# A convolution branch rewritten: Toeplitz images of all lags, or a chunked scan of states

## The chip, the cores and the metric

The kernel runs on one core of one Trainium2 chip. A core has a matrix engine (PE, with its weight loads PEld shown apart), a vector engine (DVE), a scalar engine (ACT), a general engine (POOL) and a queue engine that issues transfers (SP). 16 DMA engines move data between HBM and the on-chip memory SBUF; PE writes its results to the small memory PSUM. The metric is the time of one execution on the device in microseconds (us), here a median of three runs. The profile is taken of one execution by the hardware's own profiler.

## The reference

A forward pass and its gradients, of two branches that read the same x and are mixed by a gate. Branch a is attention with 32 heads of 18; branch b is a convolution over the 2048 tokens, channel by channel, whose kernel K is a sum of 128 complex exponentials:

```python
def _B_ref(u, A_re, A_im, B_re, B_im, C_re, C_im, log_dt, Dskip):
    dt = jnp.exp(log_dt)[:, None]
    logdA = dt * A                       # A = A_re + 1j * A_im, 576 channels x 128
    dB = dt * Bc
    P = jnp.exp(logdA[:, :, None] * l[None, None, :])      # l = 0 .. 2047
    K = jnp.einsum("dn,dnl,dn->dl", Cc, P, dB).real
    ...                                  # y = causal convolution of K and u, by FFT
    y = (lambda x, *d: x.transpose(*d))(y, 0, 2, 1) + u * Dskip[None, None, :]
    return y

x = A_x
g = _sigmoid((x * gate_w).sum(-1, keepdims=True))
a = _A_ref(x, A_wqkv, A_wo)
b = _B_ref(x, B_A_re, ...)
return g * a + (1 - g) * b
```

What is returned is this output and the gradient for each of the twelve inputs other than B_u. For branch b, with gy = (1 - g) * grad_out, that means: y from K and x; dx, the same convolution run backwards over gy; dK, the correlation of gy with x at each lag; and from dK the gradients of A, B, C and log_dt, which need two sums for each of 576 x 128 states: of dK times the exponential (S0) and of dK times lag times the exponential (S1).

## The kernel before, in words

The program is written with a framework that allocates tiles from pools, adds the semaphores, and orders each engine's instructions by its own planning; only attention has its order written out by hand. Each pool is closed before the next stage's is opened, so that stages take the same SBUF one after the other. All transfers are issued from SP's queue, in order. `mm` (line 30) is the helper behind nearly all matmuls, so they all have line 30.

The stages, by their pools:

- s1 and attention (lines 93 to 491), projections and their gradients (lines 496 to 632). The weight wo is loaded once, in s1, and kept.
- Parameters (lines 681 to 752): dt, A, B and C are transposed so that a state index lies on each partition and a channel in each column; W = C * B * dt and G, the 128th power of the state's factor, are computed; A * dt, once in its own units and once in turns, goes to a DRAM table `ath_d`.
- HX (lines 754 to 818), the gradient of the lags. gy is reversed within each 128 tokens into `GYREVp`, x is reversed and stored to `xpR_d`. For each of the 576 channels `HX`, a 128 x 2048 Toeplitz image of x, is read back from DRAM with overlapping rows (512 KB), and 16 matmuls with 128 x 128 weights and 16 columns accumulate dK for all 2048 lags.
- E (lines 820 to 941), in 36 groups of 16 channels. `abuf` and `thb` (1 MB each) bring A * dt to all partitions; ACT and DVE make the real and imaginary part of the exponential for 128 lags, `E1e` (partition = lag, 16 x 128 columns for each part). PE transposes it (line 889), ACT copies the result out (line 890). Kernel values at lag l + 128 * k are made by two matmuls a channel against a table of W times G to the power k (`Rre`, `Rni`), are transposed and stored to `Kpad_d`. `Vps` multiplies E1e with dK; a 16-step scan in G (lines 926 to 936) makes S0 and S1.
- HK (lines 943 to 994), the outputs. For each channel `HK`, a 128 x 2048 Toeplitz image of K, is read from DRAM (512 KB); each of its 16 blocks serves two matmuls of 16 columns, one for y, one for dx.
- Final (lines 996 to 1104): gradients of the parameters, then two loops over the 16 token tiles for the output and for dx.

The tiles abuf, thb, mag, uk, frac and frac2 of stage E come from a pool with one buffer each; E1e and E1n have two.

Of the kernel before, what the change touches and what calls it, by code (L numbers as in the profile page):

```python
# [17 lines left out]
P = 128  # L18


def build(tc, aps, dbg_aps=None, stages=("s1", "attn", "post", "s4", "final")):
# [39 lines left out]
    with ExitStack() as gctx:  # L61
# [14 lines left out]
        wo_sb = const.tile([P, DC, D], BF, name="wo_sb")  # L76
# [16 lines left out]
        with ExitStack() as ctx:  # L93
# [395 lines left out]
        if "post" in stages:  # L489
# [6 lines left out]
            with ExitStack() as ctx:  # L496
# [3 lines left out]
                OT = pa.tile([P, DC, S], BF, name="OT")  # L500
                cnt = 0
# [132 lines left out]
        if "s4" in stages:  # L634
# [3 lines left out]
            L = S  # L638
            NB = L // P
            LP = L + 2 * P  # L640
            NL1 = L // P
            GS = 16
            NGS = D // GS
            CG = 32
            NCG = D // CG
            HG = 128
            GPB = HG // GS
            INV2PI = float(1.0 / (2.0 * np.pi))
            Kpad_d = dram.tile([D, LP], BF, name="Kpad_d")
            xpR_d = dram.tile([D, LP], BF, name="xpR_d")  # L650
            ath_d = dram.tile([2, D, N], F32, name="ath_d")
            dkk_d = dram.tile([P, D * 2 * NL1], BF, name="dkk_d")
            dkk_v = dkk_d.rearrange("p (d a b) -> p d a b", d=D, a=2)
# [4 lines left out]
            Dskip_b = s4c.tile([P, D], F32, name="Dskip_b")  # L658
            gate_b = s4c.tile([P, D], F32, name="gate_b")
# [3 lines left out]
            Wr_n = s4c.tile([P, D], F32, name="Wr_n"); Wi_n = s4c.tile([P, D], F32, name="Wi_n")  # L663
            Gr_n = s4c.tile([P, D], F32, name="Gr_n"); Gi_n = s4c.tile([P, D], F32, name="Gi_n")
            S0r = s4c.tile([P, D], F32, name="S0r"); S0i = s4c.tile([P, D], F32, name="S0i")
            S1r = s4c.tile([P, D], F32, name="S1r"); S1i = s4c.tile([P, D], F32, name="S1i")
            dDs_row = s4c.tile([1, D], F32, name="dDs_row")
            zero_bf = s4c.tile([P, P], BF, name="zero_bf")
            nc.vector.memset(zero_bf, 0.0)
# [6 lines left out]
            lidx_i = s4c.tile([P, NL1], mybir.dt.int32, name="lidx_i")  # L676
            nc.gpsimd.iota(lidx_i, pattern=[[P, NL1]], base=0, channel_multiplier=1)
            lval = s4c.tile([P, NL1], F32, name="lval")
            nc.vector.tensor_copy(lval, lidx_i)

            with ExitStack() as ctx:
                pp = ctx.enter_context(tc.tile_pool(name="s4pp", bufs=2))
                pps = ctx.enter_context(tc.tile_pool(name="s4pps", bufs=2, space=bass.MemoryType.PSUM))
                for src_ap, dst, fn in ((log_dt, dt_b, "exp"), (Dskip, Dskip_b, None), (gate_w, gate_b, None)):
                    tmpb = pp.tile([P, D], BF, tag="rowb", name="rowb")
                    row = src_ap.rearrange("(o d) -> o d", o=1)
                    nc.sync.dma_start(tmpb, row.to_broadcast([P, D]))
                    if fn == "exp":
                        nc.scalar.activation(dst, tmpb, ACT.Exp)
                    else:  # L690
                        nc.vector.tensor_copy(dst, tmpb)
# [27 lines left out]
                t1 = pp.tile([P, D], F32, tag="t1", name="t1")  # L719
                nc.vector.tensor_tensor(Wr_n, Cr_n, Br_n, op=A.mult)  # L720
                nc.vector.tensor_tensor(t1, Ci_n, Bi_n, op=A.mult)
                nc.vector.tensor_tensor(Wr_n, Wr_n, t1, op=A.subtract)
                nc.vector.tensor_tensor(Wr_n, Wr_n, dt_b, op=A.mult)
# [96 lines left out]
            with ExitStack() as ctx:  # L820
# [8 lines left out]
                for gi in range(NGS):  # L829
# [53 lines left out]
                    if gi == 0:  # L883
                        dbg("E1e0", E1e)
# [267 lines left out]
```

## Time and profile before

| | |
|---|---|
| three timed runs, median | 6802.83 us (6802.13 to 6807.21) |
| the profiled execution, its own time | 6800.58 us |
| its span, first to last instruction | 6798.7 us |
| PE busy | 4762.3 us (70%) |
| DVE busy | 4011.0 us (59%) |
| ACT busy | 3479.8 us (51%) |
| POOL busy | 101.5 us (1%) |
| moved by DMA | 827.93 MB, mean 122 GB/s |

The page's second part cuts the span into 40 equal slices of 170 us and gives a digit for each engine: its busy share in tenths. A group line reads: line, engine, operation, output<-inputs, shape, count | busy time, mean ns of one | idle time of the engine before it, and what ended it. The view of windows gives each engine's busy time in stretches of the span. A timeline line gives the start, the length, and the instruction. A row of transfers gives the size of one in KB and the median time from issue to landing.

### The profile page before, as it was taken

The page shows a single profiled execution, that of the slowest core. Times are in us where ns is not written, and L with a number is a line of the kernel's source. Part 1 is how long each engine was busy: PE and PEld are TensorE (multiplying, and loading weights), DVE is VectorE, ACT ScalarE, POOL GpSimd, SP SyncE. Part 2 cuts the span into 40 slices and gives each one's busy share as a digit, 9 for nine tenths or more (in the row PEclk, how much of TensorE's full clock was granted, in tenths as well). Part 3 has the DMA queues.
Part 4 walks back from the last instruction along what each step waited for, and adds up shares of the span by engine and source line. Part 5 has one row for each costly group of instructions (what it writes and reads, how often), then busy time and mean ns, then how long its engine had stood idle before and what let it go on. Part 6 is the DMA issues. An engine that isn't in the chain of part 4 may idle for free. (4 is left out here: it accounts for less than half of the span.)

```text
span 6798.7 us, 147781 instructions
## 1 busy us (share of the span) xinstructions
PE 4762.3 (70%) x62071; PEld 2257.4 (33%) x62071; DVE 4011.0 (59%) x7837; ACT 3479.8 (51%) x6912; POOL 101.5 (1%) x133
## 2 busy tenths in 40 slices
PE   6779999999999999999979544443322232577672
PEld 4541212121212121222167433332322231466661
DVE  4328999989898989899943500002678767200005
ACT  3347878878787878786833300001866685300001
POOL 1000000000000000000000000000000000000000
PEclk6555555555555555555578655555555555555555
DMA  2130000000001010000030399997322232599996
GB/s 82 63 105 6 6 16 12 6 22 6 22 1 27 1 26 1 17 3 4 3 121 30 95 383 380 379 381 283 115 74 73 70 109 67 210 378 377 374 371 173
DMA packets 370257, 827.93 MB, mean 122 GB/s; under 512 B 163506, under 2 KB 193332, under 8 KB 359732
## 3 DMA queue, kind: packets, MB, share of 16 engines
q1 hardware_dynamic: 369588, 818.48, 33.7%
q8 instruction: 485, 7.95, 0.5%
q14 instruction: 184, 1.51, 0.1%
HBM read 755.45 MB, written 62.92 MB: 120 GB/s over the span
## 5 line engine op out<-in xcount | busy, mean ns | idle before, releaser
L398 DVE TENSOR_TENSOR ds<-ps_P3D,eb 128x512 bf16<-128x512 f32 x2048 | 1293.3, 686 | 128.3 <-PE ps_P3D L30 83.7
L398 DVE TENSOR_TENSOR ds<-ps_P,PT 128x512 bf16<-128x512 f32 x2048 | 1288.3, 686 | 101.5 <-PE ps_P L30 97.0
L394 ACT ACTIVATE eb<-ps_P3S 128x512 bf16<-128x512 f32 x2048 | 1109.2, 596 | 259.8 <-PE ps_P3D L30 179.1
L390 ACT ACTIVATE PT<-ps_P 128x512 bf16<-128x512 f32 x2048 | 1107.8, 596 | 211.9 <-PE ps_P L30 113.4
L30 PE MATMUL ps_P3D<-VaT_g,dOaT_g 19*128 19x512 bf16 x2048 | 790.8, 593 | 16.4 <-DVE ds L398 15.8
L30 PE MATMUL ps_P<-dOaT_g,VaT_g 19*128 19x512 bf16 x2048 | 757.9, 592 | 0.0
L30 PE MATMUL ps_P<-QaT_g,KaT_g 19*128 19x512 bf16 x2048 | 676.0, 597 | 72.1 <-DMA KaT_g<-KaT_d 37.7
L30 PE MATMUL ps_P3S<-KaT_g,QaT_g 19*128 19x512 bf16 x2048 | 671.0, 597 | 31.0 <-ACT eb L394 28.5
L889 PE MATMUL pt_e<-ident_bf,E1e 128*128 128x128 bf16 x1152 | 186.5, 281 | 690.1 <-ACT E1n L890 348.8
L30 PE MATMUL dkps<-GYREVp,HX 128*128 128x16 bf16 x9216 | 343.2, 175 | 456.4 <-DMA HX<-xpR_d 456.4
L30 PE MATMUL dxps<-CXG,HK 128*128 128x16 bf16 x9216 | 545.4, 174 | 145.7 <-issue 143.3
L30 PE MATMUL accA<-PT,Vtok_g 128*32 128x512 bf16 x2048 | 625.0, 608 | 6.0 <-DMA Vtok_g<-Vtok_d 5.8
L30 PE MATMUL accB<-ds,Qtok_g 128*32 128x512 bf16 x2048 | 626.7, 608 | 0.0
L30 PE MATMUL accA<-eb,dOa 128*32 128x512 bf16 x2048 | 626.7, 608 | 0.0
L30 PE MATMUL accB<-ds,Ktok_g 128*32 128x512 bf16 x2048 | 625.2, 608 | 0.0
L30 PEld LDWEIGHTS <-HK 128*128 128x128 bf16 x18432 | 528.3, 104 | 264.8 <-DMA HK<-Kpad_d 144.2
L30 PE MATMUL yps<-CXG,HK 128*128 128x16 bf16 x9216 | 549.9, 175 | 79.5 <-DMA HK<-Kpad_d 77.5
L984 DVE CAST y_tok<-yps 128x512 bf16<-128x512 f32 x18 | 44.0, 2443 | 746.6 <-PE dxps L30 663.8
L816 DVE TENSOR_TENSOR dkk_st<-dkps,lval 128x512 bf16<-128x512 f32 x18 | 12.4, 692 | 784.8 <-DMA HX<-xpR_d 618.5
L30 PEld LDWEIGHTS <-HX 128*128 128x128 bf16 x9216 | 290.7, 105 | 509.5 <-DMA HX<-xpR_d 508.5
L986 ACT CAST dxr<-dxps 128x512 bf16<-128x512 f32 x18 | 10.5, 585 | 795.4 <-PE dxps L30 795.4
L815 ACT CAST dkk_st<-dkps 128x512 bf16<-128x512 f32 x18 | 10.5, 585 | 786.7 <-PE dkps L30 741.9
(306 smaller groups left out, 6195.1 us busy)
## 6 DMA issues: line engine op xcount, KB each, us to landing
HX<-xpR_d SPq DMA_DIRECT2D x576, 512.0 KB, 9.6
HK<-Kpad_d SPq DMA_DIRECT2D x576, 512.0 KB, 6.7
abuf<-ath_d SPq DMA_DIRECT2D x36, 1024.0 KB, 4.7
thb<-ath_d SPq DMA_DIRECT2D x36, 1024.0 KB, 4.9
x_tok<-in_A_x_dram SPq DMA_DIRECT2D x3, 2304.0 KB, 9.5
go_t<-in_grad_out_dram SPq DMA_DIRECT2D x48, 144.0 KB, 2.2
dqkv_d<-dtk SPq DMA_DIRECT2D x48, 144.0 KB, 3.6
dqkv_tok<-dqkv_d SPq DMA_DIRECT2D x1, 6912.0 KB
```

What stands on the lines that cost most here:

```text
L30: return nc.tensor.matmul(out, lhsT=lhsT, rhs=rhs, start=start, stop=stop, **kw)
L390: nc.scalar.activation(out, ps, ACT.Exp)
L394: nc.scalar.activation(out, ps, ACT.Exp)
L398: nc.vector.tensor_tensor(out, ps, e, op=A.mult)
L815: nc.scalar.copy(dkk_st[:, :, 0, :], dkps)
L816: nc.vector.tensor_tensor(dkk_st[:, :, 1, :], dkps, lval.unsqueeze(1).to_broadcast([P, CG, NB]), op=A.mult)
L889: nc.tensor.transpose(pt[:, ri, :], E1e[:, ch, ri, :], ident_bf)
L984: nc.vector.tensor_copy(y_tok[:, :, d0:d0 + CG].transpose([0, 2, 1]), yps)
L986: nc.scalar.copy(dxr, dxps)
```

## The change

The tokens are cut into 16 chunks of 128. Within a chunk, and from each chunk to the next through the 128 complex states, the convolution is computed exactly; only the first 128 lags are needed as a kernel. The convolution part is replaced whole. In order:

- Parameters. x is reversed within each chunk (a matmul with the exchange matrix J for each half of 576 columns) and stored to `xr_d`. `zpow` makes the factor z and its 128th power Z; 14 tables go to `par_d`.
- M, the first 128 lags of dK. Tokens are regrouped as 128 runs of 16. In three batches of 192 channels, `xs` gets eight copies of x, the copy dl shifted by dl partitions (eight loads, of 128 - dl partitions); masks clear what crossed a chunk's start. For each channel one matmul of 32 weight columns by 128 columns; four channels lie side by side in the array. 16 channels are evicted to `mst`, stored to `Md_d`, read back skewed (`skw`), and summed by an fp32 matmul with a selection matrix. dK goes to `DK`.
- L, in 18 blocks of 32 channels. For each half of a block `egen` makes E1e as before, with fewer tiles, and a transposing DMA makes `E1n` in place of the transposes on PE. Per channel two matmuls of E1e with 64 columns: reversed x of 16 chunks, gy of 15, both also times their lag, and dK. From the chunks' sums a recurrence in Z over 15 chunks, forwards for x and backwards for gy, makes the states `HG`. W times z times the states (`Rw`, on POOL) through E1n gives each chunk's contribution from earlier ones (`ydi`) and the 128 kernel values, which are stored to `Kp_d`. Products of states and sums (`pair`) make S0 and S1, added up on PE through an identity. In the next block's time `t0_stage` reads the 128 x 128 Toeplitz image of 32 channels and adds the part within the chunk. y and dx go to `yd_d`.
- Final reads y and dx back from DRAM, and reverses dx's tokens there.
- wo is kept in s1's pool and loaded a second time for the projection after attention.

```diff
-            wo_sb = const.tile([P, DC, D], BF, name="wo_sb")
+            wo_sb = s1.tile([P, DC, D], BF, name="wo_sb")
...
+                wo_sb = pa.tile([P, DC, D], BF, name="wo_sb2")
+                for c, (f0, fsz) in enumerate(dch):
+                    nc.sync.dma_start(wo_sb[0:fsz, c, :], wo[f0:f0 + fsz, :])
...
+                for t in range(NB):
+                    nc.sync.dma_start(x_t, x_v[:, t, :])
+                    for u in range(2):
+                        mm(psr, lhsT=J_bf, rhs=x_t[:, u * DH2:(u + 1) * DH2])
...
+                    nc.sync.dma_start(xr_d[:, t, :], xr_t)
...
+                for r_, s_ in enumerate((Zr_n, Zr_n, Zr_n, Zr_n, Zi_n, Zi_n, nz, nz, wzr, wzi, zr_n, zi_n, nwr, nwi)):
+                    nc.sync.dma_start(par_d[:, r_, :], s_)
...
-                for cg in range(NCG):
-                    for ch in range(CG):
-                        HX = pw.tile([P, L], BF, tag="HX", bufs=8, name="HX")
-                        nc.sync.dma_start(HX, src)
-                        for dl in range(NB):
-                            mm(dkps[:, ch, :], lhsT=HX[:, P * (NB - 1 - dl):P * (NB - dl)], rhs=GYREVp[:, d, dl:dl + NB],
-                               start=(dl == 0), stop=(dl == NB - 1))
...
+                for u in range(2):
+                    xs_u = po.tile([P, NSUB, SUB, DB], BF, name=f"xs{u}")
+                    nc.gpsimd.memset(xs_u[0:NSUB], 0.0)
...
+                for bi in range(D // DB):
+                    for dl in range(NSUB):
+                        nc.sync.dma_start(xs[dl:P, dl, :, :], xsub[0:P - dl, :, d0:d0 + DB])
+                    for dl in range(1, NSUB):
+                        nc.vector.tensor_scalar(xs[:, dl, :, :], xs[:, dl, :, :], msk[:, dl:dl + 1], None, op0=A.mult)
...
+                    for u in range(DB // 16):
+                        psM = pps.tile([P, 4, P], F32, tag="psM", bufs=3, name="psM")
+                        for q in range(4):
+                            for g_ in range(4):
+                                dd = u * 16 + 4 * q + g_
+                                lw = gyp[:, :, dd]
+                                mm(psM[32 * g_:32 * (g_ + 1), q, :].rearrange("p (a b) -> p a b", b=SUB), lhsT=lw,
+                                   rhs=xs[:, :, ::-1, dd], tile_position=(0, 32 * g_))
+                        mst = mst2[(bi * (DB // 16) + u) % 3]
+                        nc.scalar.copy(mst[:, :, 0:P], psM)
+                        for g_ in range(4):
+                            nc.sync.dma_start(dst[g_], mst[32 * g_:32 * g_ + SUB, :, :])
+                        for v in range(2):
+                            nc.sync.dma_start(skw, src)
+                            mm(dst_, lhsT=skw, rhs=sel)
...
-                        for ri in range(2):
-                            nc.tensor.transpose(pt[:, ri, :], E1e[:, ch, ri, :], ident_bf)
-                        nc.scalar.copy(E1n[:, ch, :, :], pt)
...
+                    for h in range(CB // GS):
+                        E1e = egen(d0 + h * GS)
+                        nc.sync.dma_start_transpose(out=E1n[:, h * GS:(h + 1) * GS, :, :].rearrange("p c r n -> p (c r) n"),
+                                                    in_=E1e.rearrange("p c r n -> p (c r n)"))
+                        for q in range(GS // 8):
+                            for c_ in range(8):
+                                mm(pr[:, :, c_], lhsT=E1e[:, ch, 0, :], rhs=rhs)
+                                mm(pi[:, :, c_], lhsT=E1e[:, ch, 1, :], rhs=rhs)
+                            nc.scalar.mul(UV[:, 0, :, c0:c0 + 8], pr, -1.0)
+                            nc.scalar.copy(UV[:, 1, :, c0:c0 + 8], pi)
...
+                    for k in range(1, NS):
+                        nc.vector.tensor_tensor(tz, HG[:, :, k - 1, :].unsqueeze(1).to_broadcast([P, 2, 4, CB]), ZZ, op=A.mult)
+                        nc.vector.tensor_tensor(t1v, t1v, UVk[:, :, :, k, :], op=A.add)
+                        nc.vector.tensor_tensor(HG[:, 0:2, k, :], tz[:, 0, 0:2], tz[:, 1, 2:4], op=A.add)
+                        nc.vector.tensor_tensor(HG[:, 2:4, k, :], tz[:, 0, 2:4], tz[:, 1, 0:2], op=A.add)
...
+                    for s in range(2):
+                        wa = pw.tile([P, 2, NS, CB], F32, tag="wa", bufs=1, name="wa")
+                        for ri in range(2):
+                            nc.gpsimd.tensor_tensor(wa[:, ri], hv[:, ri], par[:, 8, :].unsqueeze(1).to_broadcast([P, NS, CB]), op=A.mult)
+                            nc.gpsimd.tensor_tensor(wb[:, ri], hv[:, ri], par[:, 9, :].unsqueeze(1).to_broadcast([P, NS, CB]), op=A.mult)
...
+                            mm(ybp[:, :, c_], lhsT=E1n[:, ch, 0, :], rhs=Rw[:, 0, :, ch], start=True, stop=False)
+                            mm(ybp[:, :, c_], lhsT=E1n[:, ch, 1, :], rhs=Rw[:, 1, :, ch], start=False, stop=True)
...
+                    nc.sync.dma_start(Kp_d[d0:d0 + CB, P:2 * P], KT)
...
+                    pA = pair("pA", V0, hR, NS)
+                    pB = pair("pB", V1, hR, NS)
+                    pC = pair("pC", U1, gR, NS)
...
-                        HK = pw.tile([P, L], BF, tag="HK", bufs=6, name="HK")
-                        nc.sync.dma_start(HK, src)
-                        for dl in range(NB):
-                            mm(yps[:, ch, :], lhsT=lw, rhs=CXG[:, d, 2 * NB - dl:3 * NB - dl], start=(dl == 0), stop=(dl == NB - 1))
-                            mm(dxps[:, ch, :], lhsT=lw, rhs=CXG[:, d, dl:dl + NB], start=(dl == 0), stop=(dl == NB - 1))
...
+                    if prev is not None:
+                        t0_stage(prev)
...
+                    nc.sync.dma_start(y_t, yd_d[:, 0, t, :])
...
+                    nc.sync.dma_start(dxr_t, yd_d[:, 1, NT - 1 - t, :])
```

More of the change, by code (lines that the diff above doesn't have):

```diff
@@ L683, in build @@
                 pps = ctx.enter_context(tc.tile_pool(name="s4pps", bufs=2, space=bass.MemoryType.PSUM))
[L684 to L691, printed above, removed]
+                with nc.allow_non_contiguous_dma(reason="gate values regrouped by 16 tokens"):
+                    nc.sync.dma_start(omg_d.rearrange("(t p) -> p t", p=P), omg_t)
@@ L997, in build @@
+                t0_stage(prev)
         if "final" in stages and "s4" in stages:
```

575 lines of the change are left out of this document (295 added, 280 removed).

## The prediction

> **What bounds the kernel now.** I read the page's busy times in 40 slices first, then the stage windows, then the groups by line.
>
> ```profile
> span 6798.7 us, 147781 instructions
> PE   6779999999999999999979544443322232577672
> DVE  4328999989898989899943500002678767200005
> ACT  3347878878787878786833300001866685300001
> DMA  2130000000001010000030399997322232599996
> ```
>
> The reader is to see three things. Up to slice 22 (one is 170 us) PE, DVE and ACT share the work and the DMA engines are nearly idle: that is attention and its projections, which the diff leaves alone. Then the DMA row shows two plateaus of nines, and between them, with DMA at 2 and 3, DVE and ACT stand at 6 to 8. Those are the three stages of the convolution branch. The window view prices them; its columns are the stretch, its length, the busy time of PE, PEld, DVE, ACT and POOL (instructions in brackets), the granted clock, the DMA share and GB/s:
>
> ```profile
> 3784.00:3907.00 123.00, 58.22 (x733) 38.48 (x734) 72.23 (x211) 47.16 (x154) 0.00 (x0) 0.51 0.39 116
> 3907.00:4707.00 800.00, 343.15 (x9223) 290.63 (x9220) 13.96 (x23) 11.93 (x23) 0.00 (x0) 0.50 0.98 379
> 4707.00:5748.00 1041.00, 303.69 (x4032) 265.21 (x4032) 790.65 (x1783) 695.68 (x1058) 0.00 (x0) 0.52 0.24 81
> 5748.00:6670.00 922.00, 595.92 (x18912) 549.06 (x18912) 110.95 (x169) 89.21 (x130) 0.00 (x0) 0.50 0.91 336
> 6670.00:6799.00 129.00, 10.27 (x122) 6.53 (x122) 94.74 (x179) 25.16 (x47) 0.00 (x0) 0.50 0.59 130
> HX<-xpR_d SPq DMA_DIRECT2D x576, 512.0 KB, 9.6
> HK<-Kpad_d SPq DMA_DIRECT2D x576, 512.0 KB, 6.7
> ```
>
> Parameters 123 us; gradient of the 2048 lags (HX) 800; exponentials, kernel and states (E) 1041; outputs (HK) 922; final 129: together 3015. HX and HK are bound by transfers: 576 Toeplitz images of 512 KB each, DMA share 0.98 and 0.91. E is bound by DVE (791 of 1041) with ACT close (696).
>
> **What the change removes.** Both sets of 576 images go, with their 27,648 matmuls of 16 columns, and so do E's transposes on PE and its 16-step tables. What the branch did in 3784 to 6799 is done anew by four stages, which I price in turn. Nothing of a stage overlaps much with the next: their tiles take the same SBUF, as HX, E and HK do today.
>
> **Parameters: 75 us.** The token reversal moves here (16 loads, 32 matmuls, 32 copies of 288 columns, 16 stores), the second power and the products with z add some 20 DVE operations, the 14 tables are stored (14 transfers of 288 KB), and the 192 small reversals of the old stage (L785, L787) go.
>
> ```profile
> 3822.22 0.47 SPq L759 DMA_DIRECT2D x_tok<-in_A_x_dram  x1
> L799 DVE CAST xr_st<-ps_xr 128x128 bf16<-128x128 f32 x32 | 10.2, 318 | 0.0
> L1101 DVE TENSOR_TENSOR o<-o,dxm_t 128x576 f32<-128x576 f32 x16 | 12.1, 755 | 28.8 <-DMA dxm_t<-dxm_d 28.6
> L928 DVE TENSOR_TENSOR ht<-hSr,Gr_n 128x256 f32<-128x256 f32 x60 | 25.5, 426 | 0.1
> L928 DVE TENSOR_TENSOR ht<-hSr,Gr_n 128x128 f32<-128x128 f32 x15 | 4.5, 299 | 0.0
> L853 DVE TENSOR_TENSOR pna<-Pr,Gr_n 128x64 f32<-128x64 f32 x15 | 3.3, 220 | 0.0
> ```
>
> Some 30 operations of 576 columns by 0.755 (L1101) make 22 us of DVE, beside and behind the 38 us in which the parameters come in today (3784 to SP's issue of x_tok at 3822); with the reversal beside them and the table stores behind I take 75, between 55 and 100.
>
> **Short lags (the new M stage): 222 us.** First POOL clears eight partitions of each image of x, 24,576 bf16 each, before the loads that overwrite seven of them.
>
> ```profile
> L152 POOL MEMSET Xa<- 128x16384 bf16 x2 | 27.5, 13754 | 155.6 <-PE pt_tp L200 155.6
> 462.10 2.16 SPq L287 DMA_DIRECT2D Vtok_g<-Vtok_d  x1
> L394 ACT ACTIVATE eb<-ps_P3S 128x512 bf16<-128x512 f32 x2048 | 1109.2, 596 | 259.8 <-PE ps_P3D L30 179.1 <-PE ps_P L30 32.4 <-PE ps_P3S L30 1.6
> L889 PE MATMUL pt_e<-ident_bf,E1e 128*128 128x128 bf16 x1152 | 186.5, 281 | 690.1 <-ACT E1n L890 348.8 <-DVE E1e L881 328.1 <-DVE E1e L882 11.3
> L30 PE MATMUL ps_P3D<-VaT_g,dOaT_g 19*128 19x512 bf16 x2048 | 790.8, 593 | 16.4 <-DVE ds L398 15.8
> ath_d<-adn SPq DMA_DIRECT2D x8, 64.0 KB, 1.7
> 3799.22 0.43 SPq L751 DMA_DIRECT2D xpR_d<-zero_bf  x1
> ```
>
> By L152 (0.84 ns a column) that is 21 us. A batch of 192 channels then needs eight loads of some 2048 pieces of 384 B. The timeline of SP's queue has Vtok_g: 2048 pieces of 256 B hold the queue for 2.16 us, so 17 ns a piece on each of 16 engines; 384 B lie between 17 and 25 ns, I take 21, and eight loads take 22 us. Seven masks of 3072 columns are at most 1.9 each (L871 below, 1.29 for 2048 in fp32), less in bf16, say 1: the first matmul starts 50 us in. Batches two and three load behind the work.
>
> Then come 36 rounds of 16 channels: 16 matmuls of 128 strided columns, an eviction of 512 columns (0.6, L394), four stores, two skewed loads, two fp32 matmuls. No row shows strided moving columns; the bounds are a quarter of the 512-column ps_P3D (0.15) and L889's whole 0.281, so 2.4 to 4.5 us a round, and I take 3. SP sets the round instead: the loads read what the stores wrote, so SP, in order, issues six transfers (0.43 each, L751) and waits one landing (1.7, the ath_d row): 4.3, say 4.5. Queued behind that waiting load are the next round's stores, and PE waits for them through three staging tiles. Bounds: 3 if the order lets stores pass ahead, 9 if each round is done end to end. 36 x 4.5 = 162; with 10 to drain, 222 (between 170 and 390).
>
> **States and outputs (the new L stage): 1190 us.** 18 blocks of 32 channels. The exponentials stay, twice a block:
>
> ```profile
> L871 DVE TENSOR_SCALAR uk<-thb,l0col 128x2048 f32<-128x2048 f32 x36 | 46.4, 1288 | 132.3 <-DMA thb<-ath_d 132.2
> L872 DVE TENSOR_SCALAR uk<-uk 128x2048 f32<-128x2048 f32 x36 | 44.1, 1226 | 0.8
> L874 DVE SCALAR_TENSOR_TENSOR frac<-thb,l0col,uk 128x2048 f32<-128x2048 f32 x36 | 84.6, 2350 | 1.1
> L881 DVE TENSOR_TENSOR E1e<-mag,frac 128x2048 bf16<-128x2048 f32 x36 | 82.6, 2293 | 2.5
> L869 ACT ACTIVATE mag<-abuf,l0col 128x2048 f32<-128x2048 f32 x36 | 72.1, 2002 | 18.5 <-DVE E1e L882 9.7 <-DVE E1e L881 4.9 <-DMA abuf<-ath_d 3.5
> L876 ACT ACTIVATE frac<-frac 128x2048 f32<-128x2048 f32 x36 | 68.8, 1910 | 1.8 <-DVE frac L874 1.5
> L869 ACT ACT_TABLE_LOAD x36 | 46.2, 1283 | 0.6
> L890 ACT COPY E1n<-pt_e 128x256 bf16<-128x256 bf16 x576 | 183.7, 373 | 8.4 <-PE pt_e L889 8.4
> L772 DVE TENSOR_TENSOR gx_t<-gy_tok,x_tok 128x576 bf16<-128x576 bf16 x16 | 8.4, 524 | 0.0
> L335 POOL TENSOR_TENSOR prod<-dOa,O_tok 128x288 f32<-128x288 bf16 x32 | 22.1, 690 | 2.5
> 5306.00 1.29 DVE L871 TENSOR_SCALAR uk<-thb,l0col 128x2048 f32<-128x2048 f32 x1 [6.55 <-DMA thb<-ath_d]
> 5323.88 1.29 DVE L871 TENSOR_SCALAR uk<-thb,l0col 128x2048 f32<-128x2048 f32 x1 [5.08 <-DMA thb<-ath_d]
> ```
>
> DVE, one block. Exponentials: 1.29 + 1.23 + 2.35 + 2.35 (the second product becomes a three-operand one) + 2.29 = 9.5, twice: 19.0. The recurrence: 14 steps of one 256-column product (0.426), one 128-column add (0.299) and two 64-column adds (0.220): 1.165 each, 16.3. The eight paired products of 896 to 960 bf16 columns go by L772 (0.9 ns a column, 0.8 each): 6.4, their sum of 1920 columns 1.2, the six differences of 480 columns 2.6; three-operand and output operations some 2.7, RX's share 1.2. Sum 49.4.
>
> ACT: four 2048-column functions and two table loads are 2.00 + 3 x 1.91 + 2.57 = 10.3, twice; eight evictions of 512 columns 4.8, three copies of 960 about 3, the rest 2: 30.4. The 16 copies of L890 per group are gone. POOL: ten operations of 480 columns at 690/288 = 2.4 ns: 11.5, and 28 small ones of about 0.2: 17. PE: some 250 small matmuls of 0.05 (922 us for 18,912 in HK's window) to 0.15: 13 to 38. DMA: 4 MB of broadcasts and some 10,000 small pieces: about 20. So DVE bounds.
>
> What share of the time it can be busy is the open part. In E it was busy 791 of 1041, 76%: there thb and uk have one buffer each, and from one group to the next (5306.00 to 5323.88) the chain load, phase, sine, square, product takes 18 us, with ACT's copies of L890 in its gaps. The diff keeps one buffer of each. Two chains are 36 of a block; in their gaps DVE does the recurrence and pairs of the block before, if the order on its queue has them there. 49.4 / 0.76 = 65, I take 64: 18 x 64 = 1152, and 38 for the first block's filling and the last's tail. Bounds: 52 a block (DVE nearly full) gives 975; 85 (the recurrence's 16, POOL's 11 and the pairs' 10 behind the exponentials, nothing between) gives 1570.
>
> The transposing transfer of 1024 KB, 36 times, takes L889's and L890's place; no row shows one. Downwards it is bounded by thb's load of the same size, 4.9 us in the issue list below; I take under 20 us, hidden while the block's evictions and recurrence (over 20 us) run. Its upper bound is a rival's.
>
> ```profile
> thb<-ath_d SPq DMA_DIRECT2D x36, 1024.0 KB, 4.9
> ```
>
> **Final: 165 us.** Per token tile one more load in the first loop, two more in the second, and there a scaling, a product and two 288-column additions more, about 2 us of DVE by 16: 129 + 36. The second load of wo hides behind the O_tok transposes, which it isn't needed for; without that cover it costs its 4.4.
>
> ```profile
> wo_sb<-in_A_wo_dram SPq DMA_DIRECT2D x4, 144.0 KB, 4.4
> L507 PE MATMUL pt_o<-ident_bf,O_tok x80: 263/266/316, 3416.0 to 3443.0; 128*128 128x128 bf16 x64, 128*64 128x128 bf16 x16
> ```
>
> **The sum** against the profiled execution: 3784 + 75 + 222 + 1190 + 165 = 5436. Around its span of 6798.7 that execution took 6800.6, and the three timed runs have a median of 6802.8, so 2 to 4 are added: **5440 us**, 20% less.
>
> **Rivals.**
>
> *Few engines carry the shifted loads.* Seven of the eight loads cover 127 down to 121 partitions; every large load of the trace covers 128. If partitions go to engines in equal shares only, 127 (a prime) falls to one engine, the others to 14, 5, 4, 3, 2 and 11. Then the first engine has 2032 + 144 + 400 + 496 + 656 + 976 + 176 + 128 = 5008 pieces a batch, 105 us at 21 ns instead of 22. Stores of a round have a share there and wait behind the next batch: 21 + 105 + 105, then 40 for the rest of batch one, 105 for batch three, 108 and 10: M 494, the sum 5710. For it: the counts. Against it: no row. The Trainium skill states this very rule (DMA: Bandwidth & Descriptors, section Why a DMA increments its semaphore by 16 and not by 1: the largest number up to 16 that divides both slowest dimensions); before's trace can neither bear it out nor refute it.
>
> *Blocks run one after the other.* 85 a block instead of 64: 5820. For it: single buffers (HG, Rw, thb, uk), a DVE queue in order. Against it: E overlapped its groups well.
>
> *Transposing transfers bound L.* Two a block do so from 32 us each. Midway between thb's 4.9 and the 71 below, at 38, a block takes 76: 5660. For it: no row prices them. Against it: thb's transfer, of the same size, lands in 4.9. The Trainium skill speaks for it in one place, 1309 ns for a 128x128 block (VectorE: DVE Perf Modes, section The three transpose paths), which for 32 in a row is an estimate of 42 us, 84 a block and 5800; and against it in another, where transposing transfers are as fast as ordinary ones (Advanced Engine Details and Errata, section X-Bar Transpose (TRN2)). No run here shows either yet.
>
> *Better overlap*: 52 a block, 5220.
>
> *Slower: the transposes go element by element.* Should each of 524,288 elements cost what a 256 B piece does (2.16 us for 2048), one takes 553 us and 36 take 19,900: 24,000 in all. It decides from (1363 + 1190) / 36 = 71 us a transfer. Against it: nothing but the purpose of the instruction.
>
> **Chances.** Forecast 0.38, few engines 0.32, serial blocks 0.09, transposes bounding 0.05, better overlap 0.11, element by element 0.05. The range takes in all but the last, and but few engines with serial blocks together (6090): 5150 to 5950. A measurement can tell about 0.2% here. Faster 0.94, same 0.01, slower 0.05.
>
> **What would show it.** The last HX and HK rows gone; L's start near 4080 (few engines: near 4350, DMA share low while M waits); the first DVE L-block to the last 18 x 64 us with DVE near 75%; a transposing transfer landing in under 20 us. I am wrong if PE waits for strided matmuls, or if L's DVE share is under 60%.

## The result and the profile after

| | before | after |
|---|---|---|
| median of the timed runs | 6802.5 us | 5778.1 us |
| span of the profiled execution | 6798.7 us | 5777.8 us |
| ratio, with its 95% interval | | 0.8495 (0.848 to 0.8509) |

The time fell by 15.1% where 20% was forecast (5440). 5778 lies inside the range of 5150 to 5950, but nearer to the rival of few engines (5710) than to the likeliest case. The profile page of the kernel after, its busy times in 40 slices (one is 144 us):

```profile
span 5777.8 us, 90570 instructions
PE   6687999999999999999999987832222222222221
DVE  4334899898998989989899973330017667776668
ACT  3336788787887778878788562310004444444421
DMA  2122000101001010010000013032235444444436
```

Both plateaus of nines in the DMA row are gone. In their place stand three slices (28 to 30) in which nothing is busy for more than 3 tenths, DVE and ACT at 0 or 1, PE at 2 and DMA at 2 or 3: that is M. Behind them nine slices of DVE at 6 and 7 are L. The windows of the kernel after, by the four stages of the prediction (columns as before):

```profile
3785.00:3851.00 66.00, 17.72 (x64) 5.38 (x62) 33.78 (x79) 18.76 (x45) 0.24 (x3) 0.53 0.54 166
3851.00:4319.00 468.00, 93.39 (x720) 62.70 (x720) 34.51 (x40) 22.76 (x38) 46.89 (x10) 0.53 0.26 66
4319.00:5617.00 1298.00, 296.33 (x4482) 269.19 (x4482) 900.73 (x1618) 529.66 (x520) 458.85 (x702) 0.53 0.47 113
5617.00:5778.00 161.00, 21.64 (x154) 9.71 (x154) 124.17 (x250) 25.27 (x47) 0.00 (x0) 0.50 0.70 176
```

| stage | forecast | measured | off by |
|---|---|---|---|
| parameters | 75 | 66 | -9 |
| M, short lags | 222 | 468 | +246 |
| L, states and outputs | 1190 | 1298 | +108 |
| final | 165 | 161 | -4 |

With the stage before them ending 1 us later, the four make up all of the 342 us between the sum of 5436 and the span. So there are two questions: M, where PE, the busiest engine, works for a fifth of the time, and L, where DVE is busy for as long as was forecast (900.73 / 18 = 50.0 us a block against 49.4) and the rest of a block is idle time. With the stage's filling and tail shared out over the blocks, that is 72 - 50 = 22 us (1298 / 18 = 72) where 66 - 49 = 17 was allowed for (1190 / 18 = 66).

**Where M's time is.** The timeline of DVE at M's start shows the seven masks, one for each load that covers fewer than 128 partitions; in brackets stands how long DVE was idle until that load had landed:

```profile
3916.14 1.02 DVE L824 TENSOR_SCALAR xs<-xs,msk 128x3072 bf16<-128x3072 bf16 x1 [52.44 <-DMA xs<-in_A_x_dram]
3918.75 1.02 DVE L824 TENSOR_SCALAR xs<-xs,msk 128x3072 bf16<-128x3072 bf16 x1 [1.59 <-DMA xs<-in_A_x_dram]
3926.16 1.02 DVE L824 TENSOR_SCALAR xs<-xs,msk 128x3072 bf16<-128x3072 bf16 x1 [6.40 <-DMA xs<-in_A_x_dram]
3936.11 1.02 DVE L824 TENSOR_SCALAR xs<-xs,msk 128x3072 bf16<-128x3072 bf16 x1 [8.93 <-DMA xs<-in_A_x_dram]
3948.51 1.02 DVE L824 TENSOR_SCALAR xs<-xs,msk 128x3072 bf16<-128x3072 bf16 x1 [11.38 <-DMA xs<-in_A_x_dram]
3967.34 1.02 DVE L824 TENSOR_SCALAR xs<-xs,msk 128x3072 bf16<-128x3072 bf16 x1 [17.81 <-DMA xs<-in_A_x_dram]
3971.82 1.02 DVE L824 TENSOR_SCALAR xs<-xs,msk 128x3072 bf16<-128x3072 bf16 x1 [3.46 <-DMA xs<-in_A_x_dram]
```

The masks start 2.6, 7.4, 10.0, 12.4, 18.8 and 4.5 us apart. The rival of few engines gave the loads of 126 down to 121 partitions 144, 400, 496, 656, 976 and 176 pieces on the first engine; the intervals from 126 to 122 are these counts times 18 to 20 ns, and the last is 3.3 at 19 ns and 1.1 more. On SP's queue (SPq; x9 stands for nine issues) and at PE the same stage reads so:

```profile
3872.34 95.67 SPq L822 DMA_DIRECT2D xs<-in_A_x_dram  x9
3980.01 1.89 SPq L840 DMA_DIRECT2D Md_d<-mst  x4
3982.49 1.22 SPq L846 DMA_DIRECT2D skw<-Md_d  x2
3983.75 2.08 SPq L840 DMA_DIRECT2D Md_d<-mst  x4
3983.60 1.65 PE L30 MATMUL psM<-xs,gyp 128*32 128x128 bf16 x16
```

The loads hold SP's queue itself for 96 us, so no store of a round can pass them; then the rounds follow at 3.74 us (3980.01 to 3983.75), 1.89 of it four stores and 1.22 two skewed loads. PE needs 1.65 for a round's 16 strided matmuls. The first matmuls of the three batches start at 3973, 4117 and 4265: 21 of clearing, three times 99 to 102 of loading, three times 45 to 47 of rounds and a tail of 7 are the 468.

**Where L's time is.** The waits of DVE in L's window (for what, in total, how often, the longest):

```profile
DVE Rw L973 <- POOL wa L969: 86.1, 36, 3.5
DVE yd L910 <- ACT yd L909: 74.1, 26, 6.4
DVE E1e L891 <- ACT uk L888: 73.5, 19, 7.6
DVE uk L884 <- DMA thb<-ath_d: 57.3, 13, 10.2
DVE HG L945 <- ACT UV L942: 35.9, 18, 2.7
```

`Rw` is the product that makes the outputs' weights, `yd` the sum of the outputs, `E1e` the first product of the exponentials, `uk` the first step on the phases and `HG` the start of the recurrence. No single wait holds the 400 us of idle time. One stretch of DVE's and SP's timelines shows how they hang together (thb, the phases, has one buffer):

```profile
4811.37 1.64 DVE L973 SCALAR_TENSOR_TENSOR Rw<-wa,wb 128x480 bf16<-128x480 f32 x1 [3.49 <-POOL wa L969]
4812.93 3.28 DVE L891 SCALAR_TENSOR_TENSOR E1e<-uk,abuf 128x2048 bf16<-128x2048 f32 x1
4819.61 1.63 DVE L973 SCALAR_TENSOR_TENSOR Rw<-wa,wb 128x480 bf16<-128x480 f32 x1 [3.40 <-POOL wa L969]
4831.83 2.29 DVE L892 TENSOR_TENSOR E1e<-thb,abuf 128x2048 bf16<-128x2048 f32 x1
4844.98 1.29 DVE L884 TENSOR_SCALAR uk<-thb,l0col 128x2048 f32<-128x2048 f32 x1 [5.01 <-DMA thb<-ath_d]
4857.42 2.29 DVE L891 SCALAR_TENSOR_TENSOR E1e<-uk,abuf 128x2048 bf16<-128x2048 f32 x1 [7.51 <-ACT uk L888]
```

```profile
4834.15 5.45 SPq L930 DMA_TRANSPOSE E1n<-E1e  x1
4839.64 0.58 SPq L881 DMA_DIRECT2D thb<-ath_d  x1
```

The first product of the exponentials runs at 4812.9, the second (L892), which frees thb, only at 4831.8: on DVE's queue another wait for POOL and the paired products stand between. Then SP issues the transposing transfer for 5.45 us and only behind it the next load of thb; DVE waits for that until 4845, works 5 us on the phases, and waits 7.5 for ACT's sine and its square, with nothing left to fill the gap, since the paired products are already done. The second product stands 18.9 us behind the first seven times in L, in every other block from the fourth to the sixteenth; in all other groups it is 2.2 to 2.5.

### The profile page after: what moved, and what is told of

The parts are those of the page before. It is cut to its first block, busy times and chain, and to the rows that moved or that the text cites. A ratio compares the mean times of both kernels' runs of the same rounds, so it can differ in the third digit from the quotient of the medians.

```text
span 5777.8 us, 90570 instructions
## 1 busy us (share of the span) xinstructions
PE 3879.6 (67%) x34473; PEld 1452.2 (25%) x34473; DVE 4022.2 (70%) x7458; ACT 3207.5 (56%) x6150; POOL 607.7 (11%) x845
## 2 busy tenths in 40 slices
DMA packets 599927, 316.83 MB, mean 55 GB/s; under 512 B 523198, under 2 KB 571520, under 8 KB 589634
## 5 line engine op out<-in xcount | busy, mean ns | idle before, releaser
L30 PE MATMUL uvr<-RX,E1e 128*128 128x64 bf16 x576 | 72.4, 291 | 647.9 <-DVE E1e L891 647.9
L30 PEld LDWEIGHTS <-E1e 128*128 128x128 bf16 x1152 | 119.8, 124 | 724.3 <-DVE E1e L891 629.4
L333 POOL TENSOR_TENSOR dOa<-dO_g,rl 128x288 bf16<-128x288 bf16 x32 | 21.5, 673 | 2663.7 <-DVE rl L327 2663.7
L824 DVE TENSOR_SCALAR xs<-xs,msk 128x3072 bf16<-128x3072 bf16 x21 | 21.4, 1020 | 375.9 <-DMA xs<-in_A_x_dram 375.9
L30 PEld LDWEIGHTS <-dOa 128*32 128x32 bf16 x2048 | 107.4, 101 | 634.6 <-issue 634.6
L837 ACT COPY mst<-psM 128x512 f32<-128x512 f32 x36 | 22.1, 613 | 438.4 <-PE psM L30 362.2
L30 PEld LDWEIGHTS <-Vtok_g 128*32 128x32 bf16 x2048 | 106.6, 101 | 585.1 <-issue 577.7
L30 PE MATMUL psM<-xs,gyp 128*32 128x128 bf16 x576 | 54.7, 550 | 259.8 <-DMA xs<-in_A_x_dram 133.6
L30 PEld LDWEIGHTS <-KaT_g 19*128 19x128 bf16 x2048 | 104.9, 99 | 480.6 <-issue 452.0
L30 PE MATMUL ybp<-Rw,E1n 128*128 128x31 bf16 x1152 | 71.4, 233 | 224.9 <-POOL Rw L972 219.5
```

Of the source, the lines that this page charges most:

```text
L30: return nc.tensor.matmul(out, lhsT=lhsT, rhs=rhs, start=start, stop=stop, **kw)
L333: nc.gpsimd.tensor_tensor(da[:, :, :, 0:DH], dOv, rlb, op=A.mult)
L824: nc.vector.tensor_scalar(xs[:, dl, :, :], xs[:, dl, :, :], msk[:, dl:dl + 1], None, op0=A.mult)
L837: nc.scalar.copy(mst[:, :, 0:P], psM)
```

## The experiments

Times are medians; the kernel after stands at 5778.1. Each gain is against it unless said.

**Two kernels on M's loads.** The first splits each load, the second keeps the counts and takes the shift away.

```diff
-  nc.sync.dma_start(xs[dl:P, dl, :, :], xsub[0:P - dl, :, d0:d0 + DB])
+  nc.sync.dma_start(xs[16:P, dl, :, :], xsub[16 - dl:P - dl, :, d0:d0 + DB])
+  nc.sync.dma_start(xs[dl:16, dl, :, :], xsub[0:16 - dl, :, d0:d0 + DB])
```

> Each shifted load of x is made as two: 112 partitions (16 to 127) and the rest (15 down to 9 partitions). Few-engine theory (a load of n partitions goes to as many engines as the largest divisor of n up to 16): 112 pieces an engine at 19 ns, 2.1 us, and 16 pieces more for the rest, so a batch's eight loads take 20 to 25 us instead of 96, three batches save some 215, M goes from 467 to 250 and the time from 5778 to 5560 (5540 to 5590). Rival, the shift itself is slow (other addresses for source and target, pieces of 384 B): nothing changes, 5770 to 5790.

```diff
-  nc.sync.dma_start(xs[dl:P, dl, :, :], xsub[0:P - dl, :, d0:d0 + DB])
+  nc.sync.dma_start(xs[dl:P, dl, :, :], xsub[dl:P, :, d0:d0 + DB])
```

> The loads keep their counts of 127 down to 121 partitions but read unshifted rows (the lag between x and the gradient is left out of the computation). Few-engine theory: the counts alone matter, so the load of 127 partitions still holds 38 to 39 us and the time stays at 5778 (5760 to 5795). Rival, the shift is slow: the loads of a batch fall to 20 to 25 us and the time to 5560.

Measured: 5578.6 with the split (-199.5), 5784.9 without the shift (one execution). The window of M with the split, and the first two masks without the shift:

```profile
3852.00:4114.00 262.00, 93.75 (x720) 62.07 (x720) 52.11 (x38) 22.75 (x38) 50.02 (x10) 0.56 0.55 118
```

```profile
3913.61 1.02 DVE L824 TENSOR_SCALAR xs<-xs,msk 128x3072 bf16<-128x3072 bf16 x1 [52.32 <-DMA xs<-in_A_x_dram]
3916.09 1.02 DVE L824 TENSOR_SCALAR xs<-xs,msk 128x3072 bf16<-128x3072 bf16 x1 [1.46 <-DMA xs<-in_A_x_dram]
```

M is 262 instead of 468, with more transfers of the same bytes. Without the shift the wait for the load of 127 partitions is 52.32 against 52.44: the counts set it, not the rows that are read. The target still starts 1 to 7 partitions in, but that is not what costs: the load of 121 partitions, shifted furthest, took 4.5 us. The Trainium skill's rule (DMA: Bandwidth & Descriptors, section Why a DMA increments its semaphore by 16 and not by 1), which names 127 partitions as a case of one engine, agrees with both runs. The split does not hide the loads of the second and third batch: from their first issue (3953.5 and 4030.4) to the first matmul of the batch (3984.4 and 4060.5) PE still waits for most of 31 and 30 us.

**POOL's products on DVE.** Ten operations of 480 columns a block leave POOL (the expectation counts nine); of their three lines one is shown.

```diff
-  nc.gpsimd.tensor_tensor(wa[:, ri], hv[:, ri], ..., op=A.mult)
+  nc.vector.tensor_tensor(wa[:, ri], hv[:, ri], ..., op=A.mult)
```

> The nine products and differences of 480 columns that POOL makes for a block's outputs go to DVE. Theory that POOL is part of L's pace: DVE's waits for POOL (86 us in all, 4.8 a block) go, the tenth product on DVE (1.64 us beside POOL's work) and the paired products (up to 1.64 instead of 0.66) get shorter by 3.5 a block, and nine operations of 0.65 come in, 5.8: 70 a block becomes 67.5, the time 5735 (5710 to 5755). Rival, DVE's busy time is the pace and its waits only move: 5.8 less 3.5 more a block, 5820 (5800 to 5840).

Measured: 5684.7 (-93.4), twice the expected gain. What had not been sized is how much POOL lengthens DVE's instructions. The groups by line, of the kernel after and then of this one (busy time in all, mean ns of one):

```profile
L973 DVE SCALAR_TENSOR_TENSOR Rw<-wa,wb 128x480 bf16<-128x480 f32 x36 | 58.9, 1636 | 86.1 <-POOL wa L969 86.1
L999 DVE TENSOR_TENSOR pB<-UV,hR 128x960 bf16<-128x960 bf16 x36 | 44.5, 1257 | 0.0
L999 DVE TENSOR_TENSOR pA<-UV,hR 128x960 bf16<-128x960 bf16 x36 | 41.8, 1177 | 10.6 <-ACT hR L958 10.6
```

```profile
L973 DVE SCALAR_TENSOR_TENSOR Rw<-wa,wb 128x480 bf16<-128x480 f32 x36 | 23.3, 647 | 0.0
L999 DVE TENSOR_TENSOR pB<-UV,hR 128x960 bf16<-128x960 bf16 x36 | 21.9, 647 | 0.0
L999 DVE TENSOR_TENSOR pA<-UV,hR 128x960 bf16<-128x960 bf16 x36 | 23.3, 647 | 0.0
```

The same instructions take 0.647 us without POOL's products, and 1.2 to 1.6 on average beside them. These three rows alone give back 77 of the 117 us that 180 operations of 0.65 bring in. So DVE's busy time in L went from 901 to 905 only, and the 86 us of waits for POOL are gone, while those for the sine rose from 73.5 to 110.3. The edit also changed the order on DVE's queue: here the second product of the exponentials follows the first after 2.2 to 2.5 us in every group, never after 18.9. The 93 us thus hold both effects, and this run does not tell them apart.

**Paired products left out.** `pair(...)` over one chunk instead of 15, and the sums behind it likewise.

> Of the paired products for the parameter gradients only one chunk of 15 (or 14) is made, so their sums are incomplete: DVE has some 10.5 us less a block (products 7.8, sum 1.1, differences 2.4, less what one chunk costs). If DVE's queue sets L's pace, the block goes from 70 to 59 to 61 and the time to 5580 to 5620. Rival, the chain of the exponentials with one buffer of thb and uk sets it and the paired products lie in its gaps: under 3 a block, 5720 to 5778.

Measured: 5713.8 (one execution; -64, 3.6 a block). A line of the profile page gives the busy times of the whole execution, of the kernel after and then of this one:

```profile
PE 3879.6 (67%) x34473; PEld 1452.2 (25%) x34473; DVE 4022.2 (70%) x7458; ACT 3207.5 (56%) x6150; POOL 607.7 (11%) x845
PE 3846.7 (67%) x32997; PEld 1418.6 (25%) x32997; DVE 3935.6 (69%) x7458; ACT 3188.0 (56%) x6136; POOL 555.0 (10%) x845
```

The time is far from the theory and a little better than the rival gave, but the run does not decide between them, because the 10.5 us that both start from did not go. DVE's busy time fell by 87 us, in L from 900.7 to 817.4, which is 4.6 a block, and three quarters of that came back as time. The small products still stand beside POOL's: products of 64 columns take from 0.18 to 1.2 us and average 0.62 to 0.69, as long as the 960 columns take without POOL's products. DVE's waits for thb rose to 83.0 us from 57.3. That DVE's queue in L is not full is shown by its idle 31%, not by this run.

**The transposing transfer made an ordinary one.**

```diff
-  nc.sync.dma_start_transpose(out=E1n[...], in_=E1e...)
+  nc.sync.dma_start(E1n[:, h * GS:(h + 1) * GS], E1e)
```

> In place of each transposing transfer an ordinary one of the same megabyte from and to the same tiles, so the outputs' exponentials are left untransposed. Theory of the prediction, the transposing transfer is hidden: no change, 5778 (5766 to 5790). Rival, its 4.9 us on SP's queue stand between E1e and the next load of thb, which is on the path where DVE waits for thb (13 waits, 57 us): issue 0.6 instead of 4.9, 5700 to 5750.

Measured: 5801.2 (one execution), outside both ranges. The issue takes 0.48 us instead of 4.9, and DVE's waits for thb fell from 57.3 to 46.0 only, while its waits for the load of the reversed x rose from 5.4 to 38.8. So the transposing transfer's time on SP's queue is not what holds L up by itself. The run is no clean proof that the transfer is hidden, since what stands behind it on the queues came in another order.

**The order alone.** The body of the function for a group's exponentials under `with tc.high_priority():`, nothing else.

> Nothing but the order: the exponentials of a group are given to the engines' queues ahead of other work that is ready. Theory, order of DVE's queue: in every other block the second product of the exponentials stands behind POOL's results and the paired products (ready at 4812.8, run at 4831.8), and with it the load of thb for the next group is late; 12 to 15 us in each of nine pairs of blocks go, 5778 becomes 5650 (5630 to 5690). Rival, DVE's waits for POOL and ACT set the pace whatever the order: 5760 to 5790.

**Two buffers of thb.**

```diff
-  thb = pw.tile([P, GS, N], F32, tag="thb", bufs=1, name="thb")
+  thb = pw.tile([P, GS, N], F32, tag="thb", bufs=2, name="thb")
...
-  E1e = pw.tile([P, GS, 2, N], BF, tag="E1e", name="E1e")
+  E1e = pw.tile([P, GS, 2, N], BF, tag="E1e", bufs=1, name="E1e")
```

> Two buffers for thb, for which E1e has one instead of two. Theory, the single buffer of thb sets the pace (a load that waits for the last product, then SP's 4.9 us, then 5 of landing): these go, the load lies a group ahead, 5690 (5650 to 5720). Rival, the order of DVE's queue alone does: the waits for thb (57 us) move to the sine or to POOL, 5760 to 5790; and if E1e's single buffer makes the next product wait for the transposing transfer it is slower, over 5800.

**Order and POOL's products together.**

> POOL's products on DVE (5685 when done alone, 93 us less) together with the changed order. If the two take away different waits, 93 and some 125 add up: 5560 (5540 to 5600). If what POOL's removal gained was the same lateness of the second product: 5640 to 5690. With POOL idle, DVE's busy time would then be near 54 of a block of 58 to 63.

Measured: the order 5723.5 (-54.6), two buffers 5629.1 (-148.9), order with POOL's products on DVE 5546.6 (-231.5). The order is a cause, at less than half of its expected size: the second product now follows the first after 2.2 us everywhere, but it had been late seven times and not nine, and the waits moved on, with 121.1 us for thb (57.3 in the kernel after). Two buffers of thb gave the most of these edits taken alone and beat every range that was stated. It is more than the 57 us that DVE waited for thb by name: that wait fell to 32.4 and the wait for the sine from 73.5 to 9.8, so the load's lateness also stood behind the sine. And order with POOL's products gives 83 more than the two alone add up to (93 + 55). The lateness of the second product cannot be what adds up, as either edit alone removes it. With both, the wait for the sine is 5.3 us, where it was 110.3 and 34.1 with one alone; why the two help each other so much stays open.

**All three, a miss.**

> POOL's products on DVE, the exponentials first, and two buffers of thb (one of E1e) together. If the three are one lateness seen three ways, they give no more than the first two: 5546 (5530 to 5550). Theory, with the reload of thb out of the way (66 us of DVE's waits are left for it) DVE's busy time is what remains, 54 to 55 of a block of 56: L 1010 to 1030, the time 5480 to 5510.

Measured: 5634.3, 88 slower than without the second buffer of thb. The waits of DVE and of ACT in L:

```profile
DVE yd L911 <- ACT yd L910: 140.0, 18, 9.7
DVE E1e L892 <- DMA E1n<-E1e: 35.0, 17, 3.7
```

```profile
ACT UV L942 <- POOL f L1021: 238.6, 16, 15.6
```

With the order and POOL's products on DVE alone, the first of DVE's two waits was 44.9 us and ACT's 117.6. E1e has one buffer here, and the product of the next group waits 35 us for the transposing transfer that still reads it. ACT's evictions (its copies out of PSUM) wait 239 us for POOL's closing sums of an earlier block, which still read UV; behind ACT wait DVE's additions. Together the two waits grew by 130 us, and the wait for thb fell by 57, from 66.5 to 9.5: most of the 88 us. Why ACT came to wait longer for POOL's sums is not shown, and no run gave E1e its second buffer back beside two of thb.

**M's edits, and both sides together.** Loads split as above; the first eight partitions filled by one transfer from x instead of POOL's clearing; the next batch's loads between the rounds; the four stores of a round issued by ACT.

```diff
-  nc.gpsimd.memset(xs_u[0:NSUB], 0.0)
+  nc.sync.dma_start(xs_u[0:NSUB]..., bass.AP(tensor=x2.tensor, ...))
...
-      nc.sync.dma_start(dst[g_], mst[32 * g_:32 * g_ + SUB, :, :])
+      nc.scalar.dma_start(dst[g_], mst[32 * g_:32 * g_ + SUB, :, :])
...
+  if bi + 1 < D // DB and u <= NSUB:
+      load_dl(bi + 1, u) if u < NSUB else load_gy(bi + 1)
```

> M alone: loads of 112 partitions and the rest, the first rows filled by a transfer of 8 partitions instead of POOL's clearing, the next batch's loads put between the rounds, and the stores of a round issued by ACT. SP then has two issues a round where it had six. Theory, SP's issues set the pace of a round (3.75 us): first matmul 35 us in instead of 121, rounds 2.5 to 4.5, M 150 to 190 instead of 467, the time 5465 to 5505. Rival, the landing of a round's stores sets it: rounds of 3.75 and more, M 200 to 230, 5510 to 5545.

> The edits of M and of L together; the stages follow each other, so the gains should add: the time of the kernel with L's edits less what M's edits gain alone, near 5190 (5150 to 5250).

Measured: 5513.6 (-264.4), at the lower edge of the rival's span, while M, 197 us, lies between the two. Within a batch a round now takes 3.0 us (twelve evictions start from 3897.1 to 3929.7) instead of 3.74, so SP's issues were part of the pace; some 20 us are lost from batch to batch, where the gradient's load and product come last. Both sides together took 5367.1: the L edits' 5634.3 less 264.4 are 5369.9, so the stages do add. The expected 5190 was a miss because it built on the time expected of all three edits on L, not on the 5634 that they took.

**POOL's closing sums off the queues' way.** In the kernel with the order and POOL's products on DVE, SP's waits read:

```profile
SPq L926 <- POOL f L1021: 157.9, 16, 18.2
```

L926 is the load of a block's parameters; its buffer is free only when POOL's closing sums have read it, and the load of thb stands behind it in order.

```diff
+  nc.gpsimd.tensor_copy(ptl[:, 0:2, :], par[:, 0:8:4, :])
+  nc.gpsimd.tensor_copy(ptl[:, 2:4, :], par[:, 10:12, :])
+  nc.gpsimd.tensor_copy(dkc, UV[:, :, CDK:CDK + 2, :])
...
-  zr_, zi_ = par[:, 10, :], par[:, 11, :]
+  zr_, zi_ = ptl[:, 2, :], ptl[:, 3, :]
```

> POOL's products on DVE and the exponentials first, with two buffers of E1e as before, the edits of M, and one more: POOL's closing sums of a block read small copies, made early, of the parameters and of the two columns they need. Additive theory without the new part: 5546.6 less the 264.4 that M's edits gained alone, 5282 (5265 to 5300). Theory of the new part, the load of thb stands on SP's queue behind the load of the parameters, which waits for POOL's closing sums (158 us of SP's waits), and ACT's evictions wait for the same sums (118): DVE's waits for thb (66) and for the first chunk's copy (45) shrink to under half, 5200 to 5260. Rival, those waits only move to the next late one: 5282. As with two buffers of thb, an order that runs ahead of E1n's buffers could also cost: over 5300.

Measured: 5196.2 (5195.3 to 5202.7), ratio to the kernel before 0.7645 (0.7632 to 0.7657). L's window and the first of DVE's waits in it:

```profile
4047.00:5031.00 984.00, 301.21 (x4482) 268.59 (x4482) 900.40 (x1800) 525.46 (x520) 233.42 (x576) 0.54 0.62 149
DVE uk L904 <- DMA thb<-ath_d: 18.2, 4, 9.7
```

86 us less than the sum of the parts (5282), a little more than expected. Neither SP nor ACT waits for POOL's closing sums any more, and DVE's wait for the first chunk's copy is 9.9 us instead of 44.9. DVE's busy time in L is 900.4, as in the kernel after (900.73), though its make-up is another: POOL's products came in and the longer instructions went. The stage takes 984 instead of 1298. All 314 us were idle time on DVE's queue, and DVE is now busy for 92% of L. This is the fastest version of the study.

## Why the prediction was right, and where it was wrong

**The time inside the range, by the width of the range.** The forecast of 5440 was 338 us short, and three quarters of the expected gain came. The two large stages were both priced too low, so nothing made up for anything; the range held because it was drawn to hold the rivals. By the prediction's own signs the likeliest case failed: L starts at 4319 (4080 was forecast, 4350 with few engines), and DVE is busy for 69% of L instead of some 75%. L's 72 us a block lie between the 64 of the forecast and the 85 of the rival of serial blocks.

**Removed work, right.** HX and HK are gone and with them the bound of the transfers: 316.83 MB are moved instead of 827.93, and the DMA share is 0.47 in L where it was 0.98 and 0.91.

**Parameters and final, right** (66 for 75, 161 for 165).

**M's loads, wrong.** The step that failed is "eight loads take 22 us", which divides the pieces by 16 engines. It is true of the one load of 128 partitions and of none of the other seven: the loads take 99 to 102 us a batch. With it failed "Batches two and three load behind the work": the loads hold SP's queue, and all three batches wait for theirs in the open, the split ones (some 30 us) too. The rival of few engines stood beside it, at 0.32 against 0.38, and its M of 494 is near the measured 468; it was off only in the piece (19 ns, not 21) and in what overlaps (the loads hold SP, and the rounds wait whole). The trace of before had no row for either case, and the even spread got the larger chance only because every large load in that trace covers 128 partitions.

**M's rounds, roughly right.** 3.74 us for 4.5, of which SP's six issues are 3.1 (2.6 forecast) and the rest 0.6 (1.7 forecast, for one landing). In the kernel with M's edits, four of the six issues moved to ACT, a round took 3.0, so SP sets part of the pace and not all. The clearing took 20.6 for 21. The strided matmuls cost 1.65 a round, under the stated bounds of 2.4 to 4.5: they had been taken one after another. In the trace each takes some 0.55 us and 16 of them 1.65, so they overlap; four at a time use different column groups of the array, but that this is the reason was not tested.

**L's DVE sum, right in part by luck; its idle share, wrong.** 50.0 for 49.4 a block. The exponentials (19.4 for 19.0) and the recurrence (16.2 for 16.3) came as priced. But where POOL's products are on DVE, DVE's 905.39 us less the 117 of the products themselves are 43.8 a block: the work alone is smaller than the sum, and most of the rest of the 50.0 is what POOL's products add to DVE's instructions (94 us over L973, L999 and L891, 5.2 a block), which the sum did not have. The failed step is "49.4 / 0.76": the share that E reached was carried over to a stage with other neighbours. ACT was as forecast (529.66 / 18 = 29.4 for 30.4), POOL was not: 458.85 / 18 = 25.5 for 17 (14.2 for 11.5 in its products, 11.3 for 5.6 in the small sums). "So DVE bounds" put nothing for POOL, and it cost twice, by DVE's waits for its products and by longer instructions on DVE. The runs put numbers to the idle time: 93 us with POOL's products, 55 with the order, 149 with the second buffer of thb, 314 with the first two and the closing sums out of the way. The sentence "if the order on its queue has them there" was the right condition; it did not hold in seven of the 18 blocks, where the paired products run ahead of the second product of the exponentials.

**Transposing transfers, right.** Well under 20 us, and no engine waits for one in the kernel after: the first matmul on this one's E1n starts at 4904.1, after 12.7 us of waiting for POOL. Not quite hidden is its issue, 4.8 to 6.0 us on SP's queue, ahead of the next loads of thb and abuf. An issue on SP's queue in the kernel after, and windows behind it; the last two columns are the DMA share and GB/s:

```profile
4889.42 4.87 SPq L930 DMA_TRANSPOSE E1n<-E1e  x1
```

```profile
4891.00:4893.00 2.00, 0.35 (x4) 0.19 (x2) 0.66 (x1) 2.00 (x3) 2.00 (x3) 0.50 1.16 215
4893.00:4895.00 2.00, 0.00 (x0) 0.00 (x0) 1.08 (x1) 0.74 (x2) 2.00 (x2) 0.50 1.17 218
4897.00:4899.00 2.00, 0.00 (x0) 0.00 (x0) 2.00 (x3) 0.00 (x0) 2.00 (x2) 0.50 0.98 365
4899.00:4901.00 2.00, 0.00 (x0) 0.00 (x0) 1.26 (x1) 0.00 (x0) 2.00 (x2) 0.50 1.00 422
```

A megabyte at some 217 GB/s is about 5 us; the ordinary loads of thb and abuf behind it run at 365 to 422. So the 38 us of one rival and the 71 of the slower one are far off, and so is 32 times the 1309 ns of the Trainium skill (VectorE: DVE Perf Modes, section The three transpose paths); its other place (Advanced Engine Details and Errata, section X-Bar Transpose (TRN2)), as fast as ordinary transfers, is nearer, but here the rate was little more than half of theirs. The ordinary copy of the same tiles, in the experiment above, reached 377.

## What to carry to other kernels

Look at the partition count of each large load, not only at its bytes: cutting seven loads a batch into 112 partitions and the rest was worth 199 us here. When a stage's bound is taken from another stage's busy share, work out first what frees each single buffer and what stands ahead of that instruction on its queue; an engine that is "off the path" can hold a buffer, a queue slot, or slow the busy engine's own instructions. And a named wait's total is not the gain of removing it: two buffers for thb gave 149 us against 57 named, and the same edit lost 88 on top of two others, where the waits that it made longer outweighed the one that it took away.

## What the hardware showed that was not expected

DVE and POOL slow each other. In the kernel after, a product on DVE that takes 2.29 us in most groups took 3.28, and one on POOL that takes 1.2 took 3.13, where the two overlapped:

```profile
4955.21 3.28 DVE L891 SCALAR_TENSOR_TENSOR E1e<-uk,abuf 128x2048 bf16<-128x2048 f32 x1
4956.41 3.13 POOL L969 TENSOR_TENSOR wa<-HG,par 128x480 f32<-128x480 f32 x1
```

Beside these and the rows above, the first mask in the kernel with split loads took 14.43 us instead of 1.02: it started at 3879.8, and POOL's second clearing ended at 3893.4.

```profile
L828 DVE TENSOR_SCALAR xs<-xs,msk x21: 1000/1020/14433, 3879.8 to 4055.1; 128x3072 bf16<-128x3072 bf16 x21
3872.84 20.57 POOL L804 MEMSET xs<- 8x24576 bf16 x1
```

The Trainium skill (SBUF — State Buffer, section Who interferes with whom) has the two share a pair of ports that one instruction holds to its end; the 14.4 us and the 0.65 that became 1.2 to 1.6 agree with that. In L it cost DVE some 5 us a block in longer instructions, beside 4.8 of waits for POOL's products.
